# Retention attention, a dense feed-forward and a routed one on one core: the low parts move from GpSimd to VectorE, and GpSimd's descriptor scratch is 2048 bytes

## Chip, core and metric

The kernel runs on one core of a Trainium2 chip. The metric is the device time of one execution in microseconds (us), lower is better. The engines are TensorE (PE; its weight loads are listed as PEld), VectorE (DVE), ScalarE (ACT), GpSimd (POOL) and SyncE (SP, which issues most transfers).

## What is computed

The reference runs three parts one after the other (B=4, H=8, S=576, HD=64, so 2304 tokens of 512 values):

```python
scores = scale * np.matmul(q, k.transpose(0, 1, 3, 2))
Dmat = np.where(rel >= 0, gamma[:, None, None] ** rel[None, :, :], 0.0)
x = np.matmul(scores * Dmat[None], v)            # -> [2304, 512]
h = x @ w_in                                     # 512 -> 2048
x = (h * (1.0 / (1.0 + np.exp(-h)))) @ w_out     # 2048 -> 512
logits = xn @ en.T / tau                         # xn, en: rows over their norm
expert_idx = np.argmax(logits, axis=1)           # 8 experts
out[mask] = gate_w[mask, None] * (np.maximum(x[mask] @ w1[e], 0.0) @ w2[e])
```

## The kernel before

**Numbers in two parts.** TensorE multiplies in a shortened 32-bit format. To keep the precision, an operand is split into a high part (a cast by ScalarE into that format) and a low part (the number less its high part, a subtraction with two inputs in SBUF), and each product is made of three matmuls: high by high, low by high, high by low. The subtraction goes through the helper `tt` of line 137, so all low parts carry that line, and are told apart by their tiles.

**First phase.** The tokens are worked through in 6 blocks of 384 (`NB`, `TB`). A block has 16 steps f of 128 hidden columns. `l1` makes h of the step with 12 matmuls (L831 to L833), ScalarE makes sg (the silu, L836); `l1b` casts its high part gh (ScalarE, L844) and subtracts the low part gl. `l2` runs two steps later (`LAG`) and adds nine matmuls into y (L858 gh by the high half of wo, L859 gh by its low half, L860 gl by the high half). sg has two buffers, gh and gl three. The second weights w_out come as the tile wo, 128 rows of high and low halves side by side, in two buffers (`WO_BUFS`): `wo_split` casts the high half (ScalarE, L620) and subtracts the low half, from wok (even f, kept in SBUF) or wr (odd f, reloaded from HBM). Before, the engine of these low parts is chosen where they are called:

```python
gq[i, f] = l1b(g, nc.gpsimd if i < NB - 1 or f < POOL_F else nc.vector)
...
wo[i3, f3] = wo_split(f3, wr.pop((i3, f3)), nc.gpsimd if f3 % 2 and (i3 < NB - 1 or f3 < POOL_F) else nc.vector)
```

So GpSimd makes gl in blocks 0 to 4 and in the first nine steps of block 5 (89 of 96), and wo of odd f in blocks 1 to 4 and in four steps of block 5 (36 of 88). VectorE makes the rest.

**What else VectorE does.** During block 0 it turns the weights, given in 8-byte numbers, into 32-bit ones (`to_f32`, L534, L536, L538: a shift and two merges, into vw or wok), from raw tiles vraw that SyncE loads, and makes their low parts (winl, and wo of block 0). In blocks 0 to 4 the attention of later tokens runs beside the feed-forward (masks pt, a low part xlo). After each of blocks 0 to 4 `route` finds each token's expert: 24 dot products jv of 128x512 (L746) and tiny instructions of a square root (sq_*), beside the next block. The expert rows ent for them are built at the start of block 1 by ScalarE from loads er (L662). GpSimd scales some inputs of the attention (vn, qn, qr), splits three operands of the second phase, clears a table, and scatters tokens with indirect transfers.

**Second phase.** The tokens of each expert go through its two matrices, and the result rows go out with 24 indirect transfers of GpSimd (L1159). GpSimd issues 61 transfers in the whole program. Line 1257 is the program's start, line 1270 its end.

**Order.** All engines take their instructions in the order written into their queues; that order is set when the kernel is built, by a scheduler with a timeline of its own (`TileContext(nc, schedule_with_timeline_sim=True)`). The attention, the conversion and the routing are generators that `Pace` draws on between the matmuls.

Of the kernel before, what the change touches and what calls it, by code (L numbers as in the profile page):

```python
# [23 lines left out]
NT, D, F1 = B * S, 512, 2048  # L24
# [4 lines left out]
NB = NT // TB  # L29
# [70 lines left out]
def body(tc, q, k, v, w_in, w_out, emb, tau, w1, w2, cst, out):  # L100
    nc = tc.nc
# [5 lines left out]
    sub = ALU.subtract  # L107
# [5 lines left out]
    WCOST = 2 * NF1 * 2.3  # L113
    ANCHOR = 7
    ROUTE = 8
    POOL_F = 9
    PRE, OPER = 93, (94, 95)
    O1 = 5
    NCLEAR = 11
# [16 lines left out]
    def tt(eng, o, a, b_, op):  # L136
        return eng.tensor_tensor(out=o, in0=a, in1=b_, op=op)  # L137

    def r2f(ap):
        return ap.bitcast(F32)  # L140
# [291 lines left out]
    def attention(units, psum=side_psum, psum_v=side_pv):  # L432

        yield from prepare(units[0], psum)
        for n, u in enumerate(units):
            scored = u.score(psum)
            yield 0.1
            pts = []
            for a, ps in enumerate(scored):
                pts.append(u.mask(ps, a))  # L440
                yield u.cost["item"]
            u.mix(pts, psum_v)
            yield 0.3
            if n + 1 < len(units):
                yield from prepare(units[n + 1], psum)
# [71 lines left out]
    def attention_cost(units):  # L517
        return sum(u.cost["prep"] + 2 * u.cost["item"] + 0.4 for u in units)
# [5 lines left out]
    wo = {}  # L524
# [84 lines left out]
    def wo_load(f):  # L609
        if f in KEPT:  # L610
            return wok[f].bitcast(F32)
        r = spool.tile([P, D], F32, name="wr", tag="wr", bufs=2)
        wrload[0] = i = nc.sync.dma_start(r, wod[f])
        if f == ANCHOR and anchor[0] is None:
            anchor[0] = i
        return r

    def wo_split(f, r, eng):
        t = spool.tile([P, 2 * D], F32R, name="wo", tag="wo", bufs=WO_BUFS)
        lastw[0] = nc.scalar.copy(t[:, :D], r)  # L620
        tt(eng, t[:, D:], r, r2f(t[:, :D]), sub)
        return t


# [28 lines left out]
    def build_en(efb):  # L653

        en = epool[0].tile([P, E, D], F32, name="ent")
        ent.append(en)
        for e in range(E):
            er = gpool.tile([P, D], F32, name="er", tag="yr", bufs=3)
            with tc.issue_after(rawload[0].ins):
                nc.sync.dma_start(er, emb[e].partition_broadcast(P))  # L660
            yield 0.1
            nc.scalar.activation(en[:, e].rearrange("p (c k j) -> p k c j", c=4, k=4), er.rearrange("p (k c j) -> p k c j", c=4, k=4),  # L662
                                 AF.Copy, scale=efb[:, e:e + 1])
# [160 lines left out]
    def first_phase():  # L824
        gq = {}

        def l1(i, f):
            xh, xl = block_x(i)
            h = ps_h.tile([P, 512], F32, name="h", tag="h")
            for c in range(KC):  # L830
                nc.tensor.matmul(h[:, :TB], winh[f][:, c], xh[:, c], start=(c == 0), stop=False)  # L831
                nc.tensor.matmul(h[:, :TB], winh[f][:, c], xl[:, c], start=False, stop=False)  # L832
                nc.tensor.matmul(h[:, :TB], winl[f][:, c], xh[:, c], start=False, stop=(c == KC - 1))  # L833
                hook((c + 1) / 8)
            sg = gpool.tile([P, TB], F32, name="sg", tag="sg", bufs=2)
            nc.scalar.activation(sg, h[:, :TB], AF.Silu)  # L836
            return sg

        last = [None]

        def l1b(g, eng):
            gh = gpool.tile([P, TB], F32R, name="gh", tag="gh", bufs=LAG + 1)
            gl = gpool.tile([P, TB], F32R, name="gl", tag="gl", bufs=LAG + 1)
            nc.scalar.copy(gh, g)  # L844
            last[0] = tt(eng, gl, g, r2f(gh), sub)
            return gh, gl

        yps, wr = {}, {}
# [61 lines left out]
        for s in range(total + LAG):  # L910
            i, f = divmod(s, NF1)
            now[0] = s
            if s < total:
                if f == 0 and i in plan:
                    att[0] = Pace(attention(plan[i]), attention_cost(plan[i]), s, s + NF1 - 1)
                if i == 0:
                    while ready[0] < f:
                        next(wg)
                if CLEAR <= s < CLEAR + (NCLEAR + 1) // 2:
                    with tc.issue_after(wrload[0].ins):  # L920
                        for n in range(min(2, NCLEAR - 2 * (s - CLEAR))):
                            clear_slots(2 * (s - CLEAR) + n)
                if s == NF1:
                    temp.close()
                    epool.append(left.enter_context(tc.tile_pool(name="epool", bufs=1)))
                    for _ in build_en(efb):
                        pass
                g = l1(i, f)
                gq[i, f] = l1b(g, nc.gpsimd if i < NB - 1 or f < POOL_F else nc.vector)
            if s == PRE:  # L930
                presplit()
            if s in OPER:
                with tc.issue_after(last[0].ins):
                    early[0].operands(OPER.index(s))
            if s >= LAG:
                i2, f2 = divmod(s - LAG, NF1)
                while i2 == 0 and ready[1] < f2:
                    next(wg)
                l2(i2, f2)
                l2done[0] = s - LAG  # L940
                i3, f3 = divmod(s - LAG + WO_BUFS, NF1)
                if 0 < i3 < NB:
                    wo[i3, f3] = wo_split(f3, wr.pop((i3, f3)), nc.gpsimd if f3 % 2 and (i3 < NB - 1 or f3 < POOL_F) else nc.vector)
                i3, f3 = divmod(s - LAG + WO_BUFS + 2, NF1)
                if 0 < i3 < NB:
                    wr[i3, f3] = wo_load(f3)
                if f2 == NF1 - 1:
                    rows, ss, num = evac(i2, yps.pop(i2))
                    if i2 == NB - 2:
                        routers.append(Pace(chain(route(i2, rows, ss, num), early_jobs()), 25.0, s, s + ROUTE))  # L950
                    else:
                        routers.append(Pace(route(i2, rows, ss, num), 25.0, s, s + NF1 - 3))
            hook(1.0)
            if s < total and f == NF1 - 1 and att[0] is not None:
                att[0].finish()
                att[0] = None
                if i == 4:
                    right.close()
# [275 lines left out]
    def clear_slots(n):  # L1234

        rows = E * CAP // NCLEAR
        nc.sync.dma_start(xs[rows * n:rows * n + rows].rearrange("(p a) (h d) -> p (a h) d", p=P, h=2),
                          zero.unsqueeze(1).to_broadcast([P, 2 * rows // P, D // 2]))
# [15 lines left out]


# [18 lines left out]
```

## Time and profile before

| | |
|---|---|
| median of 3 runs | 836.02 us (833.25 to 837.41) |
| profiled execution | 830.88 us, span of its trace 828.9 us |
| granted TensorE clock, mean | 0.986 of full speed |
| busy in the span | PE 791.5 us, DVE 496.8, ACT 368.2, POOL 266.9 |

The span is the time from the first to the last instruction of the profiled execution. Busy time is the time in which an engine executes; the idle time before an instruction is put down to what released it. An instruction's duration includes the time in which it stands still after its start.

### The profile page before, as it was taken

The page shows a single profiled execution, that of the slowest core. Times are in us where ns is not written, and L with a number is a line of the kernel's source. Part 1 is how long each engine was busy: PE and PEld are TensorE (multiplying, and loading weights), DVE is VectorE, ACT ScalarE, POOL GpSimd, SP SyncE. Part 2 cuts the span into 40 slices and gives each one's busy share as a digit, 9 for nine tenths or more (in the row PEclk, how much of TensorE's full clock was granted, in tenths as well). Part 3 has the DMA queues.
Part 4 walks back from the last instruction along what each step waited for, and adds up shares of the span by engine and source line. Part 5 has one row for each costly group of instructions (what it writes and reads, how often), then busy time and mean ns, then how long its engine had stood idle before and what let it go on. Part 6 is the DMA issues. An engine that isn't in the chain of part 4 may idle for free.

```text
span 828.9 us, 13425 instructions
## 1 busy us (share of the span) xinstructions
PE 791.5 (95%) x4638; PEld 662.1 (80%) x4638; DVE 496.8 (60%) x1243; ACT 368.2 (44%) x730; POOL 266.9 (32%) x244
## 2 busy tenths in 40 slices
PE   8799998999999999999999999989999999999994
PEld 5586777677888888888777888978879888888883
DVE  3989984974297319631983188376765646545440
ACT  2556555333343344334323453464664545545341
POOL 3331343547534553455425455103010011011011
PEclk9699999999999999999999999999999999999998
DMA  9989765875413431232301422359487465460000
GB/s 213 207 214 274 199 182 134 273 155 115 99 64 64 114 72 64 46 82 56 82 26 53 129 75 63 78 181 306 135 251 251 127 209 175 127 215 28 1 30 30
DMA packets 164422, 107.78 MB, mean 130 GB/s; under 512 B 100710, under 2 KB 142198, under 8 KB 164352
## 3 DMA queue, kind: packets, MB, share of 16 engines
q1 hardware_dynamic: 160512, 97.42, 44.2%
q0 software_dynamic: 3840, 9.48, 3.1%
q8 instruction: 37, 0.61, 0.3%
q14 instruction: 33, 0.27, 0.1%
HBM read 84.72 MB, written 23.19 MB: 130 GB/s over the span
## 4 chain that ended last, share of the span: by engine, by line
PE 66%; DVE 12%; DMA 8%; issue 5%; SPq 4%; ACT 3%; POOL 0%; DVEq 0%; POOLq 0%; ACTq 0%
PE h L831 6%; PE y L858 6%; PE y L859 6%; PE y L860 6%; PE h L832 6%; PE h L833 5%; PE y L1152 4%; PE y L1154 4%; PE y L1153 4%; DVE jv L746 4%; PE h L1133 4%; PE h L1131 4%; PE h L1132 4%; DMA vraw<-in_moe_w_in 3%; PE pv L264 2%
## 5 line engine op out<-in xcount | busy, mean ns | idle before, releaser
L137 POOL TENSOR_TENSOR gl<-sg,gh 128x384 fp32r<-128x384 f32 x89 | 107.4, 1210 | 155.3 <-ACT gh L844 133.7
L831 PE MATMUL h<-xhi,winh 128*128 128x384 f32 x384 | 134.1, 350 | 3.0 <-ACT xhi L513 1.7
L833 PE MATMUL h<-xhi,winl 128*128 128x384 f32 x384 | 130.9, 341 | 1.1 <-DVE winl L137 1.0
L832 PE MATMUL h<-xlo,winh 128*128 128x384 f32 x384 | 130.8, 341 | 0.0
L859 PE MATMUL y<-wo,gh 128*128 128x512 f32 x288 | 114.3, 398 | 3.3 <-DVE wo L137 3.3
L860 PE MATMUL y<-wo,gl 128*128 128x512 f32 x288 | 112.9, 396 | 1.8 <-POOL gl L137 1.8
L858 PE MATMUL y<-wo,gh 128*128 128x512 f32 x288 | 111.6, 403 | 2.5 <-ACT yr L698 2.2
L746 DVE CUSTOM_DVE_ANT_0 jv<-yr,ent 128x512 bf16<-128x512 f32 x120 | 91.2, 760 | 7.4 <-ACT yr L698 7.1
L836 ACT ACTIVATE sg<-h 128x384 f32<-128x384 f32 x96 | 47.2, 492 | 108.1 <-PE h L833 96.2
L831 PEld LDWEIGHTS h<-xhi,winh 128*128 128x128 f32 x384 | 72.9, 190 | 12.7 <-issue 3.0
L137 DVE TENSOR_TENSOR wo<-wok,wo 128x512 fp32r<-128x512 f32 x48 | 39.4, 820 | 71.7 <-ACT wo L620 71.6
L832 PEld LDWEIGHTS h<-xlo,winh 128*128 128x128 f32 x384 | 72.8, 190 | 4.5 <-issue 1.2
L1131 PE MATMUL h<-x2h,h 128*128 128x352 f32 (+1 forms) x236 | 74.8, 317 | 0.7 <-ACT h L1110 0.7
L833 PEld LDWEIGHTS h<-xhi,winl 128*128 128x128 f32 x384 | 72.8, 190 | 3.3 <-DVE winl L137 2.4
L1152 PE MATMUL y<-h,gh 128*96 128x512 f32 (+1 forms) x190 | 74.5, 392 | 0.4 <-ACT gh L1136 0.4
L1132 PE MATMUL h<-x2l,h 128*128 128x352 f32 (+1 forms) x236 | 74.6, 316 | 0.0
L1154 PE MATMUL y<-h,gl 128*96 128x512 f32 (+1 forms) x190 | 73.2, 399 | 0.0
L1110 ACT CAST h<-w1r 128x512 fp32r<-128x512 f32 x62 | 38.4, 620 | 66.5 <-PE h L1132 58.7
L1159 POOL DMA_INDIRECT out<-ob,tif x12 | 13.4, 1114 | 165.5 <-ACT ob L1158 133.9
L858 PEld LDWEIGHTS y<-wo,gh 128*128 128x128 f32 x288 | 53.7, 188 | 14.6 <-issue 3.0
L859 PEld LDWEIGHTS y<-wo,gh 128*128 128x128 f32 x288 | 54.1, 188 | 13.6 <-DVE wo L137 5.0
L860 PEld LDWEIGHTS y<-wo,gl 128*128 128x128 f32 x288 | 53.9, 188 | 13.6 <-POOL gl L137 2.7
(635 smaller groups left out, 1531.8 us busy)
## 6 DMA issues: line engine op xcount, KB each, us to landing
w1r<-in_moe_w SPq DMA_DIRECT2D x32, 512.0 KB, 5.9
w2r<-in_moe_w SPq DMA_DIRECT2D x32, 512.0 KB, 5.5
wr<-wod SPq DMA_DIRECT2D x40, 256.0 KB, 2.8
vraw<-in_moe_w_in SPq DMA_DIRECT2D x32, 256.0 KB, 5.0
vraw<-in_moe_w_out SPq DMA_DIRECT2D x16, 512.0 KB, 4.0
xs<-zero SPq DMA_DIRECT2D x11, 512.0 KB, 5.8
yd<-yr SPq DMA_DIRECT2D x18, 256.0 KB, 2.2
vn<-in_v SPq DMA_DIRECT2D x16, 256.0 KB, 4.4
```

Source lines behind the costliest of these rows:

```text
L137: return eng.tensor_tensor(out=o, in0=a, in1=b_, op=op)
L746: v_.tensor_tensor_reduce(out=jv, in0=rows[j], in1=ent[0][:, e], scale=1.0, scalar=0.0, op0=ALU.mult, op1=ALU.add, accum_out=num[:, j, e:e ...
L831: nc.tensor.matmul(h[:, :TB], winh[f][:, c], xh[:, c], start=(c == 0), stop=False)
L832: nc.tensor.matmul(h[:, :TB], winh[f][:, c], xl[:, c], start=False, stop=False)
L833: nc.tensor.matmul(h[:, :TB], winl[f][:, c], xh[:, c], start=False, stop=(c == KC - 1))
L858: nc.tensor.matmul(y, gh[:, s], w[:, :D], start=(f == 0), stop=False)
L859: nc.tensor.matmul(y, gh[:, s], w[:, D:], start=False, stop=False)
L860: nc.tensor.matmul(y, gl[:, s], w[:, :D], start=False, stop=(f == NF1 - 1))
L1131: nc.tensor.matmul(h[:, :w], h1[:, c], jb.xh[:, c, :w], start=(c == 0), stop=False)
L1132: nc.tensor.matmul(h[:, :w], h1[:, c], jb.xl[:, c, :w], start=False, stop=False)
L1152: nc.tensor.matmul(y, gh[:, sl], h2, start=(f == 0), stop=False)
L1154: m = nc.tensor.matmul(y, gl[:, sl], h2, start=False, stop=(f == NF2 - 1))
```

## The change

VectorE makes the low parts in all steps: `wo_split` and `l1b` no longer take an engine. 89 subtractions gl of 128x384 and 36 subtractions wo of 128x512 leave GpSimd, whose other work stays. The program is also built with a scratch of 2048 bytes for the descriptors of GpSimd's transfers, where the default is 16384. Line numbers below line 116 are one lower after the change.

```diff
@@ -113,7 +113,6 @@
     WCOST = 2 * NF1 * 2.3
     ANCHOR = 7
     ROUTE = 8
-    POOL_F = 9
     PRE, OPER = 93, (94, 95)
     O1 = 5
     NCLEAR = 11
@@ -615,10 +614,10 @@
             anchor[0] = i
         return r
 
-    def wo_split(f, r, eng):
+    def wo_split(f, r):
         t = spool.tile([P, 2 * D], F32R, name="wo", tag="wo", bufs=WO_BUFS)
         lastw[0] = nc.scalar.copy(t[:, :D], r)
-        tt(eng, t[:, D:], r, r2f(t[:, :D]), sub)
+        tt(nc.vector, t[:, D:], r, r2f(t[:, :D]), sub)
         return t
 
 
@@ -838,11 +837,11 @@
 
         last = [None]
 
-        def l1b(g, eng):
+        def l1b(g):
             gh = gpool.tile([P, TB], F32R, name="gh", tag="gh", bufs=LAG + 1)
             gl = gpool.tile([P, TB], F32R, name="gl", tag="gl", bufs=LAG + 1)
             nc.scalar.copy(gh, g)
-            last[0] = tt(eng, gl, g, r2f(gh), sub)
+            last[0] = tt(nc.vector, gl, g, r2f(gh), sub)
             return gh, gl
 
         yps, wr = {}, {}
@@ -926,7 +925,7 @@
                     for _ in build_en(efb):
                         pass
                 g = l1(i, f)
-                gq[i, f] = l1b(g, nc.gpsimd if i < NB - 1 or f < POOL_F else nc.vector)
+                gq[i, f] = l1b(g)
             if s == PRE:
                 presplit()
             if s in OPER:
@@ -940,7 +939,7 @@
                 l2done[0] = s - LAG
                 i3, f3 = divmod(s - LAG + WO_BUFS, NF1)
                 if 0 < i3 < NB:
-                    wo[i3, f3] = wo_split(f3, wr.pop((i3, f3)), nc.gpsimd if f3 % 2 and (i3 < NB - 1 or f3 < POOL_F) else nc.vector)
+                    wo[i3, f3] = wo_split(f3, wr.pop((i3, f3)))
                 i3, f3 = divmod(s - LAG + WO_BUFS + 2, NF1)
                 if 0 < i3 < NB:
                     wr[i3, f3] = wo_load(f3)
@@ -1254,7 +1253,7 @@
 
 
 def kernel(**inputs):
-    nc = bacc.Bacc("TRN2", target_bir_lowering=False, num_devices=1)
+    nc = bacc.Bacc("TRN2", target_bir_lowering=False, num_devices=1, dynamic_dma_scratch_size=2048)
     arrays, args = {}, []
     for name in _INS:
         a = np.ascontiguousarray(inputs[name])
```

The scheduler orders the engines anew. The first place is VectorE's queue in block 0, while the weights are converted (winl_123 and winl_124 are the low parts of two successive steps of w_in). Before:

```order
L137 TENSOR_TENSOR winl_123<-vw,winh 128x512
L534 TENSOR_SCALAR vw<-vraw 128x512
L538 SCALAR_TENSOR_TENSOR vw<-vraw,vw 128x512
L137 TENSOR_TENSOR wo<-wok_112,wo 128x512
L536 SCALAR_TENSOR_TENSOR vw<-vg,vw 128x512
L137 TENSOR_TENSOR pt<-ps,cs 128x384 x2
L534 TENSOR_SCALAR vw<-vraw 128x512
L137 TENSOR_TENSOR winl_124<-vw,winh 128x512
```

After:

```order
L136 TENSOR_TENSOR winl_123<-vw,winh 128x512
L537 SCALAR_TENSOR_TENSOR wok_112<-vraw,wok_112 128x512
L533 TENSOR_SCALAR vw<-vraw 128x512
L537 SCALAR_TENSOR_TENSOR vw<-vraw,vw 128x512
L136 TENSOR_TENSOR gl<-sg,gh 128x384
L136 TENSOR_TENSOR pt<-ps,cs 128x384 x2
L533 TENSOR_SCALAR vw<-vraw 128x512
L535 SCALAR_TENSOR_TENSOR vw<-vg,vw 128x512
L136 TENSOR_TENSOR wo<-wok_112,wo 128x512
L136 TENSOR_TENSOR winl_124<-vw,winh 128x512
```

A gl stands behind winl_123 and the next conversions, ahead of the masks pt; wo of wok_112 and one merge have changed places with their neighbours, and winl_124 stands further back.

The second place is VectorE's queue during the routing of block 4, beside block 5 (num_5393 is that block's 24 sums). Before:

```order
L137 TENSOR_TENSOR sq_rb_5368<-sq_rbb_5362,sq_tb_5364 128x3
L746 ISA jv,num_5393<-yr,ent 128x512
L746 ISA num_5393 128x1
L137 TENSOR_TENSOR sq_tb_5370<-sq_rb_5368 128x3
L746 ISA jv,num_5393<-yr,ent 128x512
L746 ISA num_5393 128x1
L137 TENSOR_TENSOR sq_tb_5370<-sq_tb_5370,sq_scb_5358 128x3
L137 TENSOR_TENSOR wo<-wok_111,wo 128x512
L746 ISA jv,num_5393<-yr,ent 128x512
L746 ISA num_5393 128x1
```

After:

```order
L136 TENSOR_TENSOR sq_rb_5368<-sq_rbb_5362,sq_tb_5364 128x3
L136 TENSOR_TENSOR gl<-sg,gh 128x384
L745 ISA jv,num_5393<-yr,ent 128x512
L745 ISA num_5393 128x1
L136 TENSOR_TENSOR sq_tb_5370<-sq_rb_5368 128x3
L136 TENSOR_TENSOR wo<-wok_111,wo 128x512
L136 TENSOR_TENSOR wo<-wr,wo 128x512
L745 ISA jv,num_5393<-yr,ent 128x512
L745 ISA num_5393 128x1
L136 TENSOR_TENSOR sq_tb_5370<-sq_tb_5370,sq_scb_5358 128x3
L745 ISA jv,num_5393<-yr,ent 128x512
```

A gl and the low half of a reloaded wo (from wr) stand among the dot products, which GpSimd made before. Further on there is a gl behind every three or four dot products.

The third place is ScalarE's queue at the start of block 1, where the expert rows ent are built. Before:

```order
L662 ACTIVATE ent<-er,efb 128x4x4x32 x3
L836 ACTIVATE sg<-h 128x384
L662 ACTIVATE ent<-er,efb 128x4x4x32
L844 CAST gh<-sg 128x384
L620 CAST wo<-wok_110 128x512
L662 ACTIVATE ent<-er,efb 128x4x4x32 x2
L836 ACTIVATE sg<-h 128x384
L697 ACTIVATE yr,ss<-y 128x512
L662 ACTIVATE ent<-er,efb 128x4x4x32
L844 CAST gh<-sg 128x384
```

After:

```order
L661 ACTIVATE ent<-er,efb 128x4x4x32 x3
L835 ACTIVATE sg<-h 128x384
L843 CAST gh<-sg 128x384
L619 CAST wo<-wok_110 128x512
L661 ACTIVATE ent<-er,efb 128x4x4x32 x2
L835 ACTIVATE sg<-h 128x384
L661 ACTIVATE ent<-er,efb 128x4x4x32
L843 CAST gh<-sg 128x384
L661 ACTIVATE ent<-er,efb 128x4x4x32
L835 ACTIVATE sg<-h 128x384
L661 ACTIVATE ent<-er,efb 128x4x4x32
L696 ACTIVATE yr,ss<-y 128x512
```

The second sg, gh and wo stand ahead of the fourth ent now, and the evacuation yr of block 0 stands behind further entries ent and sg.

## Rows read from the trace of the kernel before

**Rows 1.** Stretches: from:to, length, busy us (instructions) by engine, clock, DMA, GB/s.

```profile
40.00:130.00 90.00, 84.75 (x535) 68.94 (x534) 80.24 (x157) 51.97 (x100) 30.96 (x22) 1.00 0.78 211
...
340.00:400.00 60.00, 60.00 (x372) 50.51 (x371) 21.64 (x70) 23.72 (x49) 30.15 (x31) 1.00 0.28 72
...
480.00:500.00 20.00, 19.59 (x99) 17.25 (x97) 19.48 (x51) 9.36 (x20) 11.29 (x8) 1.00 0.21 66
```

**Rows 2.** TensorE's waits: us in total, times, longest, over the span.

```profile
PE y L859 <- DVE wo L137: 3.3, 4, 1.3
PE pv L264 <- DVE pt L137: 3.2, 3, 1.4
...
PE y L860 <- POOL gl L137: 1.8, 2, 1.0
```

**Rows 3.** Groups of the low parts: busy us, mean ns, idle before by releaser.

```profile
L137 POOL TENSOR_TENSOR gl<-sg,gh 128x384 fp32r<-128x384 f32 x89 | 107.4, 1210 | 155.3 <-ACT gh L844 133.7 <-issue 15.4 <-PE pv L275 3.3
...
L137 POOL TENSOR_TENSOR wo<-wr,wo 128x512 fp32r<-128x512 f32 x36 | 49.3, 1370 | 31.6 <-ACT wo L620 31.6
...
L137 DVE TENSOR_TENSOR wo<-wok,wo 128x512 fp32r<-128x512 f32 x48 | 39.4, 820 | 71.7 <-ACT wo L620 71.6
...
L137 DVE TENSOR_TENSOR gl<-sg,gh 128x384 fp32r<-128x384 f32 x7 | 3.9, 557 | 7.6 <-ACT gh L844 7.6
...
L137 DVE TENSOR_TENSOR wo<-wr,wo 128x512 fp32r<-128x512 f32 x4 | 2.7, 681 | 5.9 <-ACT wo L620 5.9
```

**Rows 4.** Timeline, all engines, 497.2 to 501.3: start, us, engine, instruction.

```profile
497.25 0.69 DVE L746 CUSTOM_DVE_ANT_0 jv<-yr,ent 128x512 bf16<-128x512 f32 x1
...
497.34 1.75 POOL L137 TENSOR_TENSOR wo<-wr,wo 128x512 fp32r<-128x512 f32 x1 [1.49 <-ACT wo L620]
...
497.87 1.24 DVE L137 TENSOR_TENSOR sq_rb<-sq_rb,sq_tb 128x3 f32<-128x3 f32 x1
...
499.16 1.40 POOL L137 TENSOR_TENSOR gl<-sg,gh 128x384 fp32r<-128x384 f32 x1
...
499.64 1.47 DVE L137 TENSOR_TENSOR wo<-wok,wo 128x512 fp32r<-128x512 f32 x1
501.04 0.15 DVE L137 TENSOR_TENSOR sq_tb<-sq_rb 128x3 f32<-128x3 f32 x1
...
501.17 0.50 PE L859 MATMUL y<-wo,gh 128*128 128x512 f32 x1 [1.29 <-DVE wo L137]
```

**Rows 5.** Groups of VectorE between 40 and 130 us.

```profile
L538 DVE SCALAR_TENSOR_TENSOR vw<-vraw,vw 128x512 int32<-128x512 int32 x19 | 14.3, 757 | 0.0
...
L534 DVE TENSOR_SCALAR vw<-vraw 128x512 int32<-128x512 int32 x19 | 10.8, 572 | 2.6 <-DMA vraw<-in_moe_w_in 1.5 <-DMA wod<-vw 0.9
```

**Rows 6.** The tile vw on VectorE: ns min/median/max, first and last start.

```profile
L534 DVE TENSOR_SCALAR vw<-vraw x24: 410/419/1234, 17.7 to 115.2; 128x512 int32<-128x512 int32 x24
...
L538 DVE SCALAR_TENSOR_TENSOR vw<-vraw,vw x24: 644/681/1502, 21.5 to 122.5; 128x512 int32<-128x512 int32 x24
```

**Rows 7.** Timeline, all engines, 336 to 347.

```profile
337.26 1.52 POOL L137 TENSOR_TENSOR gl<-sg,gh 128x384 fp32r<-128x384 f32 x1 [2.84 <-ACT gh L844]
...
346.49 0.40 PE L860 MATMUL y<-wo,gl 128*128 128x512 f32 x1
```

**Rows 8.** Timeline of ScalarE, 122 to 142.

```profile
135.84 0.72 ACT L662 ACTIVATE ent<-er,efb 128x512 f32<-128x512 f32 x1 [4.93 <-DMA er<-in_moe_expert_emb]
```

**Rows 9.** Instructions of line 1270, the end of the program.

```profile
L1270 POOLq DRAIN  x3: 40/103/5057, 823.0 to 828.6; - x3
```

**Rows 10.** Instructions of line 1257, the start of the program.

```profile
L1257 POOLq DRAIN  x1: 184/184/184, 0.3 to 0.3; - x1
```

**Rows 11.** Line 1159, the scatters of the result: their time to landing.

```profile
DMA to landing us min/median/max: 2.1/3.9/7.4
```

**Rows 12.** Timeline of GpSimd, 815.5 to 829.

```profile
818.64 0.92 POOL L1159 DMA_INDIRECT out<-ob,tig  x1 [0.40 <-ACTq L1199]
```

**Rows 13.** Groups of GpSimd between 40 and 130 us.

```profile
L137 POOL TENSOR_TENSOR gl<-sg,gh 128x384 fp32r<-128x384 f32 x16 | 26.6, 1664 | 52.0 <-ACT gh L844 48.7 <-PE pv L275 3.3
```

## Prediction

> **What bounds the kernel now.** I read the table of stretches first. TensorE is the bound of most of the program: between 340 and 400 us, as in the other middle stretches, it is busy all of 60.00 us while VectorE works for 21.64. Two kinds of stretch differ, and both are VectorE's. Between 40 and 130 us, where block 0 also converts the dense weights, VectorE is busy 80.24 of 90 us and TensorE 84.75; at the end of the routing of block 4 (480 to 500 us) VectorE is busy 19.48 of 20 [rows 1]. The change puts more work on VectorE there, so those are the places to price. Then I read TensorE's waits: only three of its lines wait for what the change touches, y for a low part of wo (3.3 us in 4 waits), pv for a mask product pt of VectorE (3.2 in 3), y for a low part gl (1.8 in 2), together 8.3 us [rows 2]. That is the most that earlier low parts and masks can give back. Then the groups of the low parts themselves: GpSimd makes 89 gl at a mean of 1210 ns and 36 wo at 1370 ns; VectorE makes its 7 gl at 557 ns and its 4 reloaded wo at 681 ns [rows 3].
>
> **What is removed and added.** GpSimd loses 107.4 + 49.3 = 156.7 us of work. VectorE gets 89 x 0.557 = 49.6 us and 36 x 0.681 = 24.5 us, 74.1 in all [rows 3]. Something comes back, because the two engines hold each other up. The timeline shows how [rows 4]: GpSimd's wo starts at 497.34 and ends at 499.09; a tiny instruction of VectorE with two inputs in SBUF (sq_rb, 128x3) starts at 497.87, takes 1.24 us and ends at 499.11, where one of the same size at 501.04 takes 0.15. Right after, GpSimd's gl runs from 499.16 to 500.56, and VectorE's wo takes 1.47 us instead of 0.68, and the matmul at 501.17 had waited 1.29 us for it. In these 4 us VectorE lost 1.09 + 0.79 = 1.88 us to one gl and one wo of GpSimd, which on VectorE would have cost 0.56 + 0.68 = 1.24. [...]
>
> **Block 0, 40 to 130 us.** 16 gl move: +16 x 0.557 = 8.9 us on an engine with 9.8 us free. What comes back: the shift L534 takes 572 ns here against a median of 419, the merge L538 757 against 681, so 19 x 0.153 + 19 x 0.076 = 4.3 us in two groups alone [rows 5, 6]. More lies in the other groups with two inputs. At most each of the 16 holds VectorE for a whole GpSimd gl, at the mean of all of them 1.21 us [rows 3], 19.4 us. The net is between +4.6 and -10.5 us of VectorE work. +4.6 lies within the free 9.8 us. I take **0** for this place: level.
>
> **The routing stretches.** The one above is a loss of VectorE that goes. There the low parts have slack as well: a gl that GpSimd started at 337.26, as soon as ACT's cast was done, is first read by the matmul that started at 346.49, over 7 us after it was finished [rows 7]. In the new order of VectorE a gl stands behind three or so dot products jv of 0.69 us [rows 4], some 2 us, which this slack covers. I price the new place in VectorE's queue at nothing; its cover are these 7 us, and with the cover gone each gl would stop TensorE by some 2 us. The waits that go are those behind GpSimd's instructions. 1.29 us of the 8.3 is shown to be of this kind [rows 2, 4]; the others may have other causes (a mask waits for its scores too). I take a quarter of the sum, **-2.0**, bounds 0 and -8.3.
>
> **The boundary from block 0 to block 1.** ACT stood 4.93 us for an expert embedding row until 135.84, with a cast gh and a cast wo queued behind that entry [rows 8]. In the new order of ACT, sg, gh and wo come ahead of that fourth entry, while the evacuation yr comes three entries later than it did. One is a gain, the other a loss of about the same size; TensorE has slack through the second h buffer. I take **0**, bounds -2 and +2.
>
> **The scratch.** Nothing in the stretches says that a smaller scratch changes a transfer. At the end of the program, however, GpSimd's drain starts at 823.0 and takes 5.057 us, up to 0.8 us from the end of the span, while the drain at the program's start, when GpSimd had issued no transfer, takes 0.184 [rows 9, 10]. So the drain is on the path to the end. GpSimd issues 61 transfers in between. If the drain goes through what these left in the scratch, a scratch of an eighth (2048 of 16384 bytes) can hold an eighth if it was full, more if it was not. I take a quarter: 0.18 + 4.87/4 = 1.4, so **-3.7**; bounds 0 (it has nothing to do with the scratch) and -4.9 (it goes to 0.18).
>
> **Sum.** 0 - 2.0 + 0 - 3.7 = -5.7 us. The profiled execution took 830.88 us (its span 828.9, and 1.98 around it), so 825.2 there. It lies 5.14 us under the median of the runs, 836.02; the same step from the median gives **830.3 us**.
>
> **The rivals.**
> A is the sum. *B, the drain stays*: it takes 5.06 us for a reason other than the scratch, and only the waits go: 836.02 - 2.0 = 834.0. For it speaks that a drain may wait for the last scatters, which land 2.1 to 7.4 us after their issue [rows 11]; against it that the last scatter starts at 818.64 [rows 12], so at the median it has landed when the drain begins at 823.0.
> *C, the whole of the waits goes* (8.3) with the drain's 3.7: 836.02 - 12.0 = 824.0. For it speaks that GpSimd's instructions lie beside all of these places, against it that a pt also waits for its scores.
> *D, the in-order queue (slower)*: a gl at the head of VectorE's queue waits for ACT's gh and holds back the conversions, masks and dot products behind it. GpSimd, which had nothing else to do, waited 52.0 us ahead of its 16 gl between 40 and 130 us, 3.25 us each [rows 13]. VectorE has 9.8 us free there, which 16 waits of 0.61 us use up; from 0.97 us each (15.5 = 9.8 + 5.7) D cancels the forecast gain. At 1.2 us each: 19.2 - 9.8 = +9.4, less the drain's 3.7, without the gain in waits: 836.02 + 5.7 = 841.7. For it speaks that VectorE already waits 71.6 us for ACT's casts at its 48 kept wo [rows 3], so such waits do hold it; against it that in block 0 the new order puts gl behind winl of the next step, so behind a whole step of VectorE's own conversions. [...]
> *E, the smaller scratch is full*: a transfer of GpSimd waits until one before it has landed. At the tail a scatter takes 0.92 us and 0.40 passes ahead of it [rows 12], and it lands after 3.9 at the median [rows 11]; if each waits for the landing of the one before, the last two add 2 x (3.9 - 1.32) = 5.2, the drain gains nothing, and with -2.0 it is 839.2. The scatters of the routing would start later too, but nothing reads their slots until the second phase.
> *N, nothing is to be seen*: 836.0, if the waits move from one line to another and the drain stays.
>
> **How the numbers follow.** A difference of under 0.5% (4.2 us) can hardly be told from none in this kernel, whose three runs span 833.25 to 837.41. Chances: A 0.45, B 0.21, D 0.13, C 0.12, E 0.05, N 0.04. The time is A's, 830.3, with its own range 826 to 834 (half of the waits' bound more, or a drain that halves only). Faster than 831.8: 0.36 of A, all of C, 0.02 of B, 0.50. Slower than 840.2: D and 0.02 of E, 0.15. The rest, 0.35, lies between. The range for 8 in 10 reaches from 823.5 (C with its middle, leaving out its lower half, 0.05) to 840.0 (B, N and E inside, D mostly outside, 0.11).
>
> **What will show it.** In the profile of the changed kernel: GpSimd's groups gl and wo gone, VectorE's gl near 560 ns and wo near 680 in x96 and x88, L533 near 420 and L537 near 680 ns between 40 and 130 us (right if so; else something other than GpSimd's low parts slowed them). VectorE's busy time between 40 and 130 us at 76 to 86 of 90, and no wait of VectorE's gl for gh above 10 us in sum there (D if there is). Waits of TensorE for wo, pt and gl, all from VectorE now, under 6.3 us in sum; above 8.3 the step on slack is wrong. GpSimd's last drain near 1.4 us (A), near 5 (B, E); the last scatters at the same 1.4 us from each other (E if 4). The prediction fails if VectorE becomes late in block 0 or at a mask of the attention, or if the boundary to block 1 moves by more than 2 us.

## The result and the profile after

The changed kernel took 820.74 us (median of 4 runs, 819.23 to 824.87) against 835.62 of the kernel before (4 runs): a ratio of 0.9837, 95% interval 0.9802 to 0.9872, 14.9 us by the medians. Measured twice more on other chips, it was 0.9831 (0.9783 to 0.9880) and 0.9859 (0.9822 to 0.9897). The forecast was 830.3 us, range 823.5 to 840.0: faster, as forecast, but more than twice as much, and below the range. Its profiled execution took 820.12 us, its span is 818.3, against 830.88 and 828.9.

The stretches that answer to [rows 1], with the same columns:

```profile
40.00:130.00 90.00, 84.46 (x530) 68.62 (x531) 77.89 (x172) 49.97 (x97) 4.69 (x5) 1.00 0.80 213
...
340.00:400.00 60.00, 60.00 (x369) 50.14 (x368) 31.04 (x89) 24.02 (x49) 9.32 (x11) 1.00 0.28 72
...
480.00:500.00 20.00, 20.00 (x102) 18.01 (x101) 18.54 (x67) 7.97 (x15) 0.00 (x0) 1.00 0.10 27
```

VectorE carries 15 more subtractions between 40 and 130 us and is nevertheless busy for less, 77.89 us against 80.24. Between 480 and 500 us it has 18.54 against 19.48, and TensorE is busy all the time. Only in stretches that had room does VectorE's time rise (31.04 against 21.64 between 340 and 400). Where block 0 gives way to block 1, TensorE no longer stands still; before, then after:

```profile
130.00:180.00 50.00, 44.49 (x248) 33.83 (x247) 39.17 (x118) 20.77 (x46) 22.55 (x21) 1.00 0.74 204
```

```profile
130.00:180.00 50.00, 50.00 (x282) 38.36 (x281) 40.43 (x137) 24.30 (x53) 7.00 (x9) 1.00 0.70 192
```

The groups of the low parts in the whole span, and then three groups of VectorE between 40 and 130 us:

```profile
L745 DVE CUSTOM_DVE_ANT_0 jv<-yr,ent 128x512 bf16<-128x512 f32 x120 | 83.2, 693 | 1.3 <-ACT yr L697 1.1
...
L136 DVE TENSOR_TENSOR gl<-sg,gh 128x384 fp32r<-128x384 f32 x96 | 55.9, 582 | 75.3 <-ACT gh L843 66.3 <-issue 7.5 <-ACT sg L835 1.3
...
L136 DVE TENSOR_TENSOR wo<-wok,wo 128x512 fp32r<-128x512 f32 x48 | 33.8, 704 | 19.1 <-ACT wo L619 18.9
...
L136 DVE TENSOR_TENSOR wo<-wr,wo 128x512 fp32r<-128x512 f32 x40 | 30.2, 754 | 14.1 <-ACT wo L619 14.0
```

```profile
L537 DVE SCALAR_TENSOR_TENSOR vw<-vraw,vw 128x512 int32<-128x512 int32 x19 | 13.0, 685 | 0.0
...
L136 DVE TENSOR_TENSOR gl<-sg,gh 128x384 fp32r<-128x384 f32 x15 | 8.3, 551 | 0.0
L533 DVE TENSOR_SCALAR vw<-vraw 128x512 int32<-128x512 int32 x19 | 8.0, 422 | 5.5 <-DMA vraw<-in_moe_w_in 5.4
```

The shift takes 422 ns where it took 572, the merge 685 where it took 757 [rows 5]; a gl costs 551 ns here, and none of the 15 waits for its cast (idle 0.0). Rival D, the queue held up by gl in block 0, isn't there. The 66.3 us for which VectorE's gl wait for gh lie in the later blocks; TensorE waits for none of these gl.

TensorE's waits after, the first five of the view (us in total, times, longest):

```profile
PE pv L505 <- DVE xlo L136: 3.5, 2, 2.4
PE h L830 <- ACT winh L591: 2.8, 5, 0.9
PE h L830 <- ACT xhi L512: 2.6, 1, 2.6
PE h L1126 <- DVE gl L1136: 1.8, 4, 0.7
PE y L857 <- ACT wo L591: 1.8, 2, 1.1
```

The three lines of [rows 2], 8.3 us in all, are gone without a rest. So are two that the prediction had taken no account of; in the same view before:

```profile
PE y L858 <- ACT yr L698: 2.2, 2, 1.7
...
PE h L833 <- DVE winl L137: 1.0, 2, 0.9
```

Other waits are longer than before: for winh (2.8 us, 1.2 before), for xhi ahead of block 0 (2.6, 1.7 before) and for wo of L591 (1.8, none before). The last drain:

```profile
L1269 POOLq DRAIN  x3: 44/103/892, 816.6 to 818.0; - x3
```

0.892 us, where it was 5.057 [rows 9].

### The profile page after: what moved, and what is told of

The parts are those of the page before. It is cut to its first block, busy times and chain, and to the rows that moved or that the text cites. A ratio compares the mean times of both kernels' runs of the same rounds, so it can differ in the third digit from the quotient of the medians.

```text
span 818.3 us, 13340 instructions
## 1 busy us (share of the span) xinstructions
PE 790.0 (97%) x4638; PEld 661.1 (81%) x4638; DVE 518.3 (63%) x1368; ACT 368.4 (45%) x730; POOL 113.8 (14%) x119
## 4 chain that ended last, share of the span: by engine, by line
PE 77%; DMA 8%; DVE 5%; issue 4%; SPq 2%; ACT 2%; POOL 0%; POOLq 0%; DVEq 0%; ACTq 0%
PE h L830 8%; PE y L857 8%; PE y L858 7%; PE y L859 7%; PE h L831 7%; PE h L832 7%; DMA vraw<-in_moe_w_in 5%; PE y L1153 4%; PE y L1151 4%; PE y L1152 4%; PE h L1132 4%; PE h L1130 4%; PE h L1131 4%; PE pv L263 3%; PE ps L362 2%
## 5 line engine op out<-in xcount | busy, mean ns | idle before, releaser
L136 DVE TENSOR_TENSOR gl<-sg,gh 128x384 fp32r<-128x384 f32 x96 | 55.9, 582 | 75.3 <-ACT gh L843 66.3
L745 DVE CUSTOM_DVE_ANT_0 jv<-yr,ent 128x512 bf16<-128x512 f32 x120 | 83.2, 693 | 1.3 <-ACT yr L697 1.1
L1116 ACT CAST h<-w2r 128x512 fp32r<-128x512 f32 x63 | 38.8, 620 | 46.3 <-PE y L1153 45.5
L843 ACT CAST gh<-sg 128x384 fp32r<-128x384 f32 x96 | 49.3, 514 | 7.7 <-PE y L858 5.1
```

What stands on the lines that cost most here:

```text
L745: v_.tensor_tensor_reduce(out=jv, in0=rows[j], in1=ent[0][:, e], scale=1.0, scalar=0.0, op0=ALU.mult, op1=ALU.add, accum_out=num[:, j, e:e ...
```

## The experiments

A number that most of them use is the time from the start of the first silu (L836) to that of the last, read from the tile sg on ScalarE. It holds the six blocks, and neither the start of the program, where TensorE's granted clock is low (0.67 of full speed between 20 and 40 us before, 0.74 after), nor the second phase nor the drain. In the two traces it is 537.5 - 41.3 = 496.2 us before and 530.9 - 41.2 = 489.7 after; below it is called the six blocks.

**The scratch and the move apart.** The queues of these two kernels are, row by row, those of the changed kernel and of the kernel before.

```diff
# the changed kernel (move only)
-    nc = bacc.Bacc("TRN2", target_bir_lowering=False, num_devices=1, dynamic_dma_scratch_size=2048)
+    nc = bacc.Bacc("TRN2", target_bir_lowering=False, num_devices=1)
# the kernel before (scratch only)
-    nc = bacc.Bacc("TRN2", target_bir_lowering=False, num_devices=1)
+    nc = bacc.Bacc("TRN2", target_bir_lowering=False, num_devices=1, dynamic_dma_scratch_size=2048)
```

> The changed kernel with the default scratch of 16384 bytes; the queues of all engines are those of the changed kernel. Theory (two parts that add: GpSimd's last drain goes with the scratch, the rest with the low parts): the last drain is 5.1 us again and the time lies 4.2 us above the changed kernel, about 825 us, a ratio to the kernel before near 0.988. Rival 1 (the drain is short because GpSimd has less to do): drain 0.9 us, no difference to the changed kernel, ratio 0.984. Rival 2 (the smaller scratch does all of it): ratio 1.00.

> The kernel before with a scratch of 2048 bytes; the queues of all engines are those of the kernel before. Theory (two parts that add): the last drain falls from 5.06 to about 0.9 us, nothing else moves, ratio near 0.995 (-4.2 us). Rival 1 (the drain is short because GpSimd has less to do): drain 5.1 us, ratio 1.00. Rival 2 (the smaller scratch does all of it): ratio 0.984.

Measured: the move alone 829.21 us, 0.9925 (0.9896 to 0.9955); the scratch alone 830.57 us, 0.9946 (0.9925 to 0.9967). Their last drains, first with the low parts moved, then with the scratch made smaller:

```profile
L1269 POOLq DRAIN  x3: 44/103/5057, 816.7 to 822.3; - x3
```

```profile
L1270 POOLq DRAIN  x3: 40/103/892, 824.6 to 826.0; - x3
```

The drain goes with the scratch and not with GpSimd's work, and a ratio of 0.9946 is 4.5 us of 835.3, near the 4.2 that it lost. Both rivals fall. The move alone came out at 6 us, less than the 9 to 11 that are left of the whole; its eight runs fell into two groups, 824.3 to 827.3 us at a mean granted clock of 0.984 to 0.988, and 831.1 to 832.8 at 0.978 to 0.981. So it was measured again beside the changed kernel, on one chip:

> The changed kernel itself, once more beside the next one, on one chip. Theory (drain and low parts add up: the two measured apart give 4.5 + 6.1 = 10.6 us): ratio 0.987 here, the 0.984 measured first being within its interval of that. Rival (the small scratch is worth more when the low parts are on VectorE, since the changed kernel was 3 us better than the sum): 0.983 again.

> The changed kernel with the default scratch, once more. Theory (the drain alone lies between the two): 4.2 us above the changed kernel of this call, with as many slow starts. Rival (the scratch also acts elsewhere): 7 us or more above it.

Measured: 822.78 us, 0.9831 (0.9783 to 0.9880), and the move only 825.86 us, 0.9870 (0.9825 to 0.9916): 3.1 us apart, not clearly different from the drain's 4.2, and its six runs lie between 825.0 and 827.1. Within this noise the two parts add up. Why half of the first eight runs had the lower clock isn't known; the traced one belongs to the other half.

**How far executions of one kernel differ.** The kernel before, traced twice more:

> The kernel before, one more profiled execution. Theory (its executions differ in block 0, where VectorE, full by GpSimd's blocking, and the arriving weights set the pace): an execution nearer to 835 us is longer than the one shown by 3 to 5 us, nearly all of it before 140 us. Rival (a matter of the start, with TensorE's clock low for longer): the difference is there before 41 us.

> As the one before it: the kernel before, one more profiled execution; the same theory and rival.

834.02 and 840.10 us. The rows of sg in both (ns least, median, most; first and last start):

```profile
L836 ACT ACTIVATE sg<-h x96: 462/492/548, 41.6 to 540.3; 128x384 f32<-128x384 f32 x96
```

```profile
L836 ACT ACTIVATE sg<-h x96: 462/492/547, 41.8 to 545.1; 128x384 f32<-128x384 f32 x96
```

Their six blocks took 498.7 and 503.3 us, that of the run with the small scratch alone (same queues) 498.4, the one of the prediction 496.2: it was the shortest of four, whose mean is 499.2. The changed kernel's queues were traced seven times: 489.7, 488.8, 491.1, 490.0, 489.5, 491.5 and 489.9, mean 490.1. The two groups don't overlap. **The move is worth 9.1 us in the six blocks, of which one pair of traces showed 6.5, and with the drain's 4.2 this makes 13.3**, which lies within the three measured differences (11.7, 12.6 and 14.9 us by the medians). Of the 7.1 us by which the six blocks of the longest execution exceed the shortest, 3.6 were there at the first silu of block 1 and 6.1 at the ninth: it is block 0 and its boundary, as the theory had it, and the start is not it (0.2 and 0.5 us). There TensorE waited 2.6 us for winl instead of 1.0, which the shortest execution had partly been spared.

VectorE's lateness is not all of it. TensorE's granted clock is at 1.00 between 140 and 150 us in the execution of the prediction. In the one with 498.7 us, TensorE stood 2.0 us for yr at 142 to 144 us, and the mean of its clock between 140 and 150 was 0.66 of full speed. These are the rows of both (the clock is the third number from the end):

```profile
140.00:150.00 10.00, 7.94 (x39) 5.53 (x40) 8.26 (x22) 7.59 (x18) 5.36 (x5) 1.00 0.66 195
```

```profile
140.00:150.00 10.00, 7.79 (x29) 6.30 (x28) 7.12 (x17) 8.46 (x20) 6.19 (x6) 0.66 0.62 148
```

The longest execution shows 0.90 and 0.93 in the two slices from 140 to 160. How much of the differences this makes stays open: the trace with a scratch of 8192 bytes has two such slices too (0.83 from 60 to 70 and from 120 to 130), and its six blocks are no longer than the others.

**gl alone, wo alone.** Scratch 2048 in both.

```diff
# the kernel before, gl only
-                gq[i, f] = l1b(g, nc.gpsimd if i < NB - 1 or f < POOL_F else nc.vector)
+                gq[i, f] = l1b(g, nc.vector)
# the kernel before, wo only
-                    wo[i3, f3] = wo_split(f3, wr.pop((i3, f3)), nc.gpsimd if f3 % 2 and (i3 < NB - 1 or f3 < POOL_F) else nc.vector)
+                    wo[i3, f3] = wo_split(f3, wr.pop((i3, f3)), nc.vector)
```

> The gl of all steps on VectorE, the 36 wo still on GpSimd; scratch 2048. Theory (what is gained beside the drain are TensorE's waits behind low parts of GpSimd, and every instruction that leaves GpSimd gives its share): 89 of 125 instructions and 107 of 157 us leave, so about two thirds of the 6.4 us, ratio about 0.990 with the drain. Rival (the wo alone were the late ones, since most of the waits are y for wo and one gl only in block 0): ratio 0.994, the drain alone.

> The 36 wo on VectorE, the gl of 89 steps still on GpSimd; scratch 2048. Theory (every instruction that leaves gives its share): a third of the 6.4 us beside the drain, ratio about 0.992. Rival (the wo alone were the late ones): ratio 0.987, as the changed kernel or nearly.

gl alone: 820.46 us, 0.9812 (0.9788 to 0.9836), as fast as the whole change. wo alone: 825.92 us, 0.9877 (0.9850 to 0.9904). Beside the drain's 4.2 us, that is some 11 and 6 us where the whole has 9: the shares don't add, and the theory's thirds are wrong. gl was set beside the whole once more, on one chip:

> The gl of all steps on VectorE, the 36 wo still on GpSimd, scratch 2048, once more. Theory (the instructions' shares don't add: with the gl gone, GpSimd's wo seldom meet anything that TensorE waits for): within 2 us of the changed kernel beside it. Rival (each has its share): 3 us or more above the changed kernel, which the first measurement missed by the difference of the chips.

> The changed kernel beside gl alone: 820 to 823 us by both theories, as twice before.

821.52 us (0.9842, 0.9802 to 0.9883) and 823.89 (0.9859, 0.9822 to 0.9897), six blocks 489.8 and 489.9. Once the gl are gone, the 36 wo on GpSimd cost TensorE nothing that is seen in the time, though they still slow VectorE down and are waited for now and then:

```profile
L746 DVE CUSTOM_DVE_ANT_0 jv<-yr,ent 128x512 bf16<-128x512 f32 x120 | 88.4, 736 | 1.7 <-ACT yr L698 1.3
...
L137 POOL TENSOR_TENSOR wo<-wr,wo 128x512 fp32r<-128x512 f32 x36 | 49.9, 1387 | 157.8 <-ACT wo L620 157.8
```

```profile
PE y L859 <- POOL wo L137: 1.1, 2, 0.6
```

jv takes 736 ns (693 without them, 760 with all). So no worth of the wo part is seen beside that on gl (821.52 without it, 823.89 with it, their intervals overlap). No version here beats the changed kernel by more than its interval.

**Which gl.** The changed kernel, with those of block 0 on GpSimd again, or all but those (and the 36 wo).

```diff
# block 0 back
-                gq[i, f] = l1b(g)
+                gq[i, f] = l1b(g, nc.gpsimd if i == 0 else nc.vector)
# the rest back, wo as in the kernel before
-                gq[i, f] = l1b(g)
+                gq[i, f] = l1b(g, nc.gpsimd if 0 < i < NB - 1 or i and f < 9 else nc.vector)
```

> The changed kernel with the 16 gl of block 0 on GpSimd again. Theory (about two thirds of what TensorE gained lie in block 0 and at its boundary, where its steps of the traces differ by 4.4 us): 4 us slower than the changed kernel, ratio near 0.988, and winl or gl waited for again. Rival (the gain is in the later blocks, in the routing): as the changed kernel, 0.983.

> The changed kernel with the 73 gl of blocks 1 to 5 and the 36 wo on GpSimd again; block 0 keeps its gl on VectorE. Theory (what the later blocks gained is a third, some 2.5 us, at the mask near 421 us and in the routing near 500 us): ratio near 0.986. Rival (the gain is in the later blocks): 0.992 to 0.995.

Block 0 back: 824.99 us, 0.9865 (0.9830 to 0.9900), six blocks 493.0. The rest back: 833.06 us, 0.9949 (0.9922 to 0.9975), six blocks 504.8. The first went the way of the theory, but how far is not certain: its six blocks are 2.9 us longer than the changed kernel's mean of 490.1 (the traced run, 828.19, was the longest of six), and its median lies 1 to 4 us above the three of the changed kernel, within their intervals. TensorE waits 2.0 us for winl and 0.7 for a gl again, and in block 0 the conversions are slow again (two groups of VectorE between 40 and 130 us):

```profile
L537 DVE SCALAR_TENSOR_TENSOR vw<-vraw,vw 128x512 int32<-128x512 int32 x20 | 15.0, 755 | 0.0
...
L533 DVE TENSOR_SCALAR vw<-vraw 128x512 int32<-128x512 int32 x19 | 9.8, 523 | 3.7 <-DMA wod<-vw 2.2 <-DMA vraw<-in_moe_w_in 1.4
```

The second went to the rival. With gl of block 0 alone on VectorE nothing is gained but the drain: the six blocks of the traced run were even longer than in any trace of the kernel before (at 838.15 us it was the longest of its twelve). Three of TensorE's waits there:

```profile
PE y L858 <- DVE wo L136: 3.7, 3, 2.2
...
PE y L858 <- POOL wo L136: 3.0, 2, 2.3
PE y L859 <- POOL gl L136: 2.4, 1, 2.4
```

Here GpSimd's own results come late too (y for its wo 3.0 us, for its gl 2.4), besides those of VectorE. What a stretch gains can't be read as a share of the whole; that it depends on what the scheduler makes of the rest is likely, but not shown.

**GpSimd's work without a reader.** This takes the lateness of GpSimd's results out and leaves its blocking. `extra` holds for the steps whose low part GpSimd made before; junk is a tile of its own.

```diff
             last[0] = tt(nc.vector, gl, g, r2f(gh), sub)
+            if extra:
+                tt(nc.gpsimd, junk[:, :TB], r2f(gh), cs[:, :TB], sub)
...
         tt(nc.vector, t[:, D:], r, r2f(t[:, :D]), sub)
+        if extra:
+            tt(nc.gpsimd, junk, r2f(t[:, :D]), cs[:, :D], sub)
```

> The changed kernel, in which GpSimd gets its 89 + 36 subtractions back, of the same sizes, but of gh or the high half of wo and of a constant, into a tile that nobody reads; the low parts stay on VectorE. Theory (TensorE waited because GpSimd's instructions hold up VectorE's that have two inputs in SBUF): VectorE's durations grow again (jv from 0.69 towards 0.76 us, L537 from 0.685 towards 0.75 between 40 and 130 us), waits of TensorE for wo, pt or winl come back, and the time rises by 5 to 9 us, to 826 to 830. Rival (TensorE waited because GpSimd's low parts themselves came late, 1.2 us instead of 0.56 each, behind others in GpSimd's queue): nobody waits for the tile, so the time stays at 820 to 822 although VectorE is slower.

837.98 us, 1.0025 (0.9998 to 1.0052), 14 to 17 us above the changed kernel, twice what was expected, although nothing reads the tile. The six blocks took 507.3 us in the traced run, which at 843.92 was the longest of its twelve. GpSimd's two groups, VectorE's groups, and TensorE's first two waits:

```profile
L136 POOL TENSOR_TENSOR junk<-gh,cs 128x384 f32<-128x384 f32 x89 | 114.1, 1282 | 149.2 <-ACT gh L846 146.7 <-DMA qn<-in_q 0.9
...
L748 DVE CUSTOM_DVE_ANT_0 jv<-yr,ent 128x512 bf16<-128x512 f32 x120 | 98.3, 819 | 0.7 <-ACT yr L700 0.5
...
L136 DVE TENSOR_TENSOR gl<-sg,gh 128x384 fp32r<-128x384 f32 x96 | 62.5, 651 | 58.0 <-ACT gh L846 58.0
L136 POOL TENSOR_TENSOR junk<-wo,cs 128x512 f32<-128x512 f32 x36 | 55.1, 1530 | 24.0 <-ACT wo L620 22.6 <-DMA qr<-in_q 0.5
...
L136 DVE TENSOR_TENSOR wo<-wok,wo 128x512 fp32r<-128x512 f32 x48 | 43.1, 898 | 11.6 <-ACT wo L620 11.3
...
L136 DVE TENSOR_TENSOR wo<-wr,wo 128x512 fp32r<-128x512 f32 x40 | 35.6, 890 | 11.6 <-ACT wo L620 11.6
```

```profile
PE y L863 <- DVE wo L136: 4.9, 4, 1.8
PE pv L264 <- DVE pt L136: 3.9, 4, 1.9
```

jv takes 819 ns (693 in the changed kernel), gl 651 (582), wo 898 and 890 (704 and 754), and TensorE waits for VectorE's wo and pt as it did before, 4.9 and 3.9 us. The rival falls as the only cause: VectorE's delay is enough for such waits. That the cost is larger than in the kernel before, since VectorE makes the low parts as well, is likely and not shown (the traced execution also has a granted clock of 0.96 between 40 and 130 us and 0.94 between 130 and 180); ScalarE's casts also waited 2.3 us for the unread subtractions, which hold a buffer of wo. The queues are ordered otherwise than in the changed kernel, so a control was run in which GpSimd gets 89 added instructions that read nothing:

```diff
-            gl = gpool.tile([P, TB], F32R, name="gl", tag="gl", bufs=LAG + 1)
+            glw = gpool.tile([P, 1024], F32R, name="gl", tag="gl", bufs=LAG + 1)
+            gl = glw[:, :TB]
+            if extra:
+                nc.gpsimd.memset(r2f(glw), 0.0)
```

> The changed kernel, in which GpSimd sets a tile of 128x1024 (the one whose first 384 columns gl is then written to) to zero ahead of 89 of the 96 gl: work that reads nothing from SBUF. Theory (only GpSimd's reading holds up VectorE's instructions with two inputs in SBUF): VectorE's durations stay near those of the changed kernel (jv 0.69, gl 0.58 us) and the time stays within 821 to 824 us. Rival (any work of GpSimd does it, or the order that goes with it): durations as in the run with unread subtractions (jv 0.82, gl 0.65) and 830 us or more.

830.50 us, 0.9927 (0.9897 to 0.9958), six blocks 498.0. The durations of VectorE's instructions with two inputs are those of the changed kernel, with 85 us of GpSimd's work beside them; behind the groups stand VectorE's waits for the memsets, the longest of them, and the only wait of TensorE between 130 us and the last silu:

```profile
L845 POOL MEMSET gl<- 128x1024 f32 x89 | 84.7, 957 | 227.5 <-PE y L862 208.4 <-DVE st L136 7.9 <-DVE ex L758 4.5
L745 DVE CUSTOM_DVE_ANT_0 jv<-yr,ent 128x512 bf16<-128x512 f32 x120 | 82.6, 689 | 1.2 <-ACT yr L697 1.0
...
L136 DVE TENSOR_TENSOR gl<-sg,gh 128x384 fp32r<-128x384 f32 x96 | 56.9, 593 | 84.3 <-ACT gh L846 58.9 <-POOL gl L845 18.6 <-issue 4.4
```

```profile
DVE gl L136 <- POOL gl L845: 18.6, 8, 4.6
```

```profile
194.15 1.38 DVE L136 TENSOR_TENSOR gl<-sg,gh 128x384 fp32r<-128x384 f32 x1 [4.63 <-POOL gl L845]
```

```profile
PE rp L765 <- DVE pt L136: 3.2, 1, 3.2
```

The timelines say it for single instructions. A jv with nothing of GpSimd beside it took 0.68 us; beside a GpSimd instruction with two inputs 0.83 in the kernel before (63 of 120) and 0.99 in the run with unread subtractions (55 of 120); beside a memset 0.68 again, at most 0.69 (35 of 120). So in these runs it is GpSimd's reading that slows VectorE's instructions with two inputs, not its presence. The shift L533, which has one input, is not spared: it took 0.58 us beside a memset (7 cases, up to 1.14) and 0.42 with nothing beside it.

The time lies 7 to 10 us above the changed kernel, where the theory had put it beside it: the memset has to go ahead of gl, and gl waited 18.6 us for it in 8 places, a wait that this control brought in. TensorE's waits tell the two runs apart. From 130 us to the last silu it stands still 8.1 us in the kernel before, not at all in the changed kernel, 7.8 us with the unread subtractions, all of it for VectorE's pt and wo, and 3.2 us with the memsets, in one wait for a pt that stood behind the gl of 194.15. The rest of the control's time is not divided up: its traced execution has a granted clock of 0.95 between 40 and 130 us and of 0.94 between 180 and 240, where the changed kernel has 1.00 in both.

**GpSimd without any products.** The 50 products vn, qn and qr go to VectorE as well (three times `tt(nc.gpsimd, t, t, ...)` becomes `tt(nc.vector, t, t, ...)`).

> The changed kernel with the 50 products vn, qn and qr of the attention on VectorE too, so that GpSimd computes almost nothing in the first phase. Theory (what GpSimd reads while VectorE works is lost on VectorE): VectorE gets some 24 us (26 x 0.68 and 24 x 0.3, from its own instructions of these sizes), and loses the rest of its delays; the start gets shorter by about 1 us; 1 to 3 us faster than the changed kernel. Rival (the in-order queue: a product waits for its transfer at the head of VectorE's queue, where GpSimd had waited 183 us for qr, and holds the conversions behind it): 5 us slower or more, with VectorE's waits for kr, qr and vn loads above 10 us in sum.

831.96 us, 0.9941 (0.9912 to 0.9970), six blocks 501.9, 8 to 11 us above the changed kernel: the rival. VectorE's waits for these loads:

```profile
DVE qr L136 <- DMA qr<-in_q: 25.7, 13, 6.3
...
DVE vn L136 <- DMA vn<-in_v: 19.3, 11, 4.1
```

25.7 and 19.3 us at the head of VectorE's queue, on which conversions and masks stand. That is what rival D had said of gl. It didn't come for gl, whose cast was done in time in block 0, and it came for products whose input is a transfer.

**The length of the drain.** The changed kernel with other scratches.

> The changed kernel with a scratch of 8192 bytes; its last drain is what is looked at. Theory (the drain goes through the whole scratch, used or not, once transfers were issued: 5.057 us at 16384 and 0.892 at 2048 lie on a line of 0.29 us per 1024 bytes): 2.68 us. Rival (it goes through what the 61 transfers left, and these filled the large scratch only in part): nearer to 5 than to 2.7.

> The changed kernel with a scratch of 6144 bytes; its last drain is what is looked at: 5.057 us at 16384 bytes, and 0.892 at 8192 and at 2048, so not a line through the size. Theory (the drain goes through what was entered since the scratch was last full; 8192 is a multiple of 2048, so the same rest is left in both; 6144 leaves another rest): not 0.892, something between 0.9 and 5. Rival (two levels: short once the scratch has been full, long if it never was): 0.892.

With 8192 bytes, then with 6144:

```profile
L1269 POOLq DRAIN  x3: 44/103/892, 818.0 to 819.4; - x3
```

```profile
L1269 POOLq DRAIN  x3: 44/103/2117, 825.7 to 828.4; - x3
```

0.892 us with 8192, as with 2048: no line through the size, and not nearer to 5, so both views held of it fall. 2.117 with 6144: not two levels either, and within the theory's 0.9 to 5. What sets the length is not shown: no run counts what was entered.

## Why the prediction was wrong

- **The mechanism was right.** GpSimd's subtractions hold up VectorE's instructions (jv 0.83 us beside them, 0.68 alone), VectorE gets no fuller where it was full (77.89 us for 80.24, 18.54 for 19.48), and TensorE's waits behind it go (8.3 us). The unread subtractions bring such waits back (7.8 us), and the control shows that it is their reading (jv 0.68 beside a memset, 0.99 beside them). One wait that went, that for yr, is of another kind (below).
- **The step that failed is "I take a quarter of the sum, -2.0".** All 8.3 us went. 5.9 of them (pt 3.2, wo 2.7) lay after 130 us, where nothing took their place: before, TensorE stood still 5.5 us between 130 and 180 us and 2.6 between 400 and 505, after the change not at all. The other 2.4 (gl 1.8, wo 0.6) lay in block 0, where waits for winh, qt and wo of L591 took their place. I had allowed only what I had seen in one timeline, 1.29 us, and held the other causes (a mask's scores) for likely with no row that showed one. Of the rivals, C, with 0.12, came nearest in mechanism and in time, though not the whole 8.3 became time.
- **Boundary of block 0, "I take 0".** The wait of y for yr (2.2 us) is missing in all seven traces of the changed kernel's queues, and there (1.8 to 2.2) in all four of the kernel before's. I had noted the place and not counted this wait. It is missing with the unread subtractions too, and there where GpSimd makes the gl of block 0 (1.6 with these back, 1.7 with wo alone moved): it goes with the engine of these gl and the order that follows from it, not with VectorE's durations. With the pt and wo that lie there, the boundary moved by 5.5 us, more than the 2 at which the prediction was to fail.
- **"Only three of its lines wait for what the change touches".** The wait for winl, a low part that VectorE makes beside GpSimd's gl in block 0, was a fourth (1.0 us, up to 2.6 in the other traces).
- **Block 0 at 0.** VectorE's 80.24 us became 77.89, within the forecast 76 to 86. The 19.4 us taken as the most that could come back were an estimate that no run shows; with the 15 gl at 8.3 us, some 10.7 came back (80.24 + 8.3 - 77.89). TensorE stands still 5.3 us between 40 and 130 before and 5.5 after, so in this pair 0 was right there. Slack and the queue of VectorE: right, TensorE waits for no wo, pt or gl of VectorE in the six blocks.
- **The scratch, -3.7.** It was -4.17, and not by the way argued (an eighth or a quarter of what fills it), since 8192 bytes give the same as 2048.
- **"The same step from the median."** The traced execution of before was the shortest of four in the six blocks, by 3.0 us under their mean, and that was luck in block 0 and at its boundary. A step read from one trace that was 5 us under its median is too small a step: the waits that the typical execution has more of are among those that the change removes. By the six blocks this put the forecast some 2.6 us (9.1 - 6.5) too high and would have brought C's 824.0 to 821.4. With the 4.5 us that TensorE's stretches were sized too small (6.5 instead of 2.0 in the pair) and the drain's 0.5, it takes 830.3 to 822.7, among the three measured medians.

## What to carry to other kernels

Where GpSimd helps VectorE with elementwise work that reads SBUF, add what VectorE's instructions lose beside it: here 156.7 us left GpSimd, by the prediction 74 us of subtractions came to VectorE, and VectorE's busy time rose by only 21.5. When a change removes one cause of several waits, price it at the whole of the waits that this cause can reach, unless a row shows another cause or another wait that is ready to take its place; and take several traces before a step of 1% is read from one. Work whose input is a transfer is better left on an engine that may wait: here 50 such products on VectorE made the kernel 8 to 11 us slower.

## What the runs showed of the hardware

GpSimd's last drain took 5.057 us with a scratch of 16384 bytes, 2.117 with 6144, and 0.892 with 8192 and with 2048, for the same 61 transfers; the drain at the start took 0.18 to 0.19 with 16384, 6144 and 2048 bytes. At the tail the smaller scratch delayed no scatter: the last three follow each other by 1.3 us after the change (1.4 before); the earlier ones were not compared.

In the kernel before, a VectorE dot product of 128x512 took 0.68 us alone and 0.83 on average beside a GpSimd instruction with two inputs; tiny instructions of the square root took 0.16 and 0.88. TensorE's granted clock had a mean of 0.66 of full speed between 140 and 150 us in the execution in which TensorE stood 2.0 us for yr there, and 1.00 in the one of the prediction.
